# Sigmoid attention with all products in steps of 64 keys of two pairs on four 64x64 parts of TensorE, in native float32, and the mixing on VectorE alone

## The chip, the cores and the metric

The kernel runs on one core of a Trainium2 chip. The metric is the device time of one execution in microseconds (us), the median of three runs. One core has TensorE (PE; its weight loads are shown as PEld), VectorE (DVE), ScalarE (ACT), GpSimd (POOL) and SyncE (SP), whose queue issues every DMA of this kernel.

## The reference

```python
# q, k, v: (8, 12, 448, 64) float32
scores = scale * np.matmul(q, k.transpose(0, 1, 3, 2)) - np.log(S)      # S = 448
attn = 1.0 / (1.0 + np.exp(-scores))
attn_out = np.matmul(attn, v)
x = attn_out.transpose(0, 2, 1, 3).reshape(B, S, H * D)                 # (8, 448, 768)
x_prev = x shifted by one position in the sequence, zeros first
xk = mu_k * x + (1.0 - mu_k) * x_prev
xr = mu_r * x + (1.0 - mu_r) * x_prev
k = np.maximum(xk @ w_k, 0.0)                                           # w_k: float64, 768 x 1024
v = k * k @ w_v                                                         # w_v: float64, 1024 x 768
r = 1.0 / (1.0 + np.exp(-(xr @ w_r)))                                   # w_r: float64, 768 x 768
out = r * v
```

The sigmoid acts on every score alone, so no row of scores has to be complete before its values are used.

## The kernel before

There are 96 heads, taken two at a time: 48 **pairs** `n`, the two heads `h` of a pair on partitions 0-63 and 64-127 of `raw` (q and k, transposed). Two pairs, `n` and `n + 1` with `n` even, are called a **couple** here; there are 24. After the attention comes the channel mix, three matrix products (`xr @ w_r`, `xk @ w_k`, `k*k @ w_v`) written with seven products of half blocks, by line 590. The first two matrices are read as raw float64 bits and made into float32 on VectorE during the attention (`convert`, lines 220 to 224; sums of blocks, line 252; for `w_r` also the split into a high and a low part, lines 297 and 298).

For one pair `n` the attention does this:

- `load`: one DMA brings q and k into `raw[n % 4]`, one brings v into `vn[n % 5]`.
- `prepare` (lines 315 and 316, VectorE): k of the first 384 keys and q are each cast to the fast format fp32r (`hi`), and the remainder `lo` is computed, into a spare part of the weight tiles `slot`.
- `scores` (line 336, TensorE): for each 128 keys and each head three products hi*hi, lo*hi, hi*lo with 64 rows and 128 columns of the array, into `sc`, a ring of three tiles of two PSUM banks.
- `sigmoid` (line 359, ScalarE): one instruction of 128x896 for each 128 keys, `sc` to `pf`, a ring of seven.
- `weigh` (line 366, TensorE): `pf` times v in native float32 with 128 rows and 64 columns, into `av`, two banks.
- The last 64 keys of both pairs of a couple are done together on four 64x64 parts of the array in native float32: `score_tails` (line 347, straight from `raw`), a sigmoid into `pt`, and `weigh_tails` (line 374).
- `gather` (lines 388 to 390): for each of `mu_r`, `mu_k` a memset on GpSimd, a multiplication of the shifted result by 1 - mu on ScalarE (389), then a multiply-add on VectorE (390) and a DMA to DRAM (`xr_d`, `xk_d`); `xo` has four tiles.

The order of all instructions is made by `Plan`: each operation has a cost and a priority, a list scheduler runs them in a model of the engines, and the program is written in the order of the start times. TensorE's operations are also chained by the resource `"order"`, so they stand as written.

Of the kernel before, what the change touches and what calls it, by code (L numbers as in the profile page):

```python
# [8 lines left out]
F32 = mybir.dt.float32  # L9
F32R = mybir.dt.float32r  # L10
AF = mybir.ActivationFunctionType
# [11 lines left out]
class Plan:  # L23
# [7 lines left out]
    def op(self, engine, cost, prio, run, reads, writes, dma=None):  # L31
        i = len(self.ops)
        deps = set()
        for r in reads:
            if r in self.writer:
                deps.add(self.writer[r])
        for w in writes:
            if w in self.writer:
                deps.add(self.writer[w])
            deps.update(self.readers.get(w, ()))  # L40
        for r in reads:
            self.readers.setdefault(r, []).append(i)
        for w in writes:
            self.writer[w] = i
            self.readers[w] = []
        deps.discard(i)
        self.ops.append(Op(engine, cost, prio, run, deps, dma))
# [51 lines left out]
def attention_then_channel_mix(  # L99
# [23 lines left out]
    NT = B * S  # L123
    NJ = DM // P
    NF = DF // P
    NC = S // P
    TAIL = S - NC * P
    KW = NC * P
    QKW = KW + S
    NV = 2 * NC + 1  # L130
    HN = DM // 2
    NJH, NFH = NJ // 2, NF // 2
    WO = NJH * DF // 2
# [21 lines left out]
    wk_o = [dram.tile([P, WO], F32, name=f"wk_o{p}") for p in range(7)]  # L155
    wv_o = [dram.tile([P, WO], F32, name=f"wv_o{p}") for p in range(7)]

    WP, PFB, RAW, WB = 512, 7, 4, 7
    SPARE = 2 * NJH * HN

    def ring(pool, name, bufs, shape, dtype):
        return [pool.tile(shape, dtype, name=f"{name}{i}") for i in range(bufs)]
# [10 lines left out]
    apool = att.enter_context(tc.tile_pool(name="apool", bufs=1, side="right"))  # L173
    ps = ExitStack()
    psum = ps.enter_context(tc.tile_pool(name="psum", bufs=1, space=PSUM))
    av = ring(psum, "av", 2, [P, 512], F32)
    sc = ring(psum, "sc", 3, [P, 2, 512], F32)

    raw = ring(apool, "raw", RAW, [P, 2 * S], F32)
    vn = ring(apool, "vn", 5, [P, NV, D], F32)  # L180
    kk = [slots[g][:, SPARE:SPARE + 2 * KW].rearrange("p (t n) -> p t n", t=2) for g in (0, 3)]
    qh = [slots[g][:, SPARE:SPARE + S] for g in (1, 4)]
    ql = [slots[g][:, SPARE:SPARE + S] for g in (2, 6)]
    pf = ring(apool, "pf", PFB, [P, 2, S], F32)
    pt = ring(apool, "pt", 2, [P, 2, S], F32)
    xo = ring(apool, "xo", 4, [P, S], F32)

    plan = Plan()
    op = plan.op
    SP, PE, ACT, DVE, POOL = "SP", "PE", "ACT", "DVE", "POOL"  # L190
    SWITCH = 200

    def mm(n, cols=S):
        return n * max(cols / 2.4 + 3.5, 205)

    def act(n, sbuf=False, ptr=False):
        return 51 + 0.834 * n + 42 * sbuf + 93 * ptr

    def dve(n, fast=False, ptr=False):
        return 69 + n / (1.92 if fast else 0.96) + 61 * ptr  # L200
# [7 lines left out]
    def dma(dst, src, prio, reads, writes):  # L208
        ns = dst.shape[0] * math.prod(dst.shape[1:]) * 4 / 300
        op(SP, 500, prio, lambda: nc.sync.dma_start(dst, src), reads, writes, dma=ns)  # L210
# [92 lines left out]
        return put  # L303

    def load(n, at):
        dma(raw[n % RAW], qk[n], at, [], [("raw", n % RAW)])
        dma(vn[n % 5], v[n], at, [], [("vn", n % 5)])

    def prepare(n, at):
        i = n % 2  # L310
        src = raw[n % RAW]
        R = ("raw", n % RAW)
        for src_, hi, lo, key in ((src[:, :KW], kk[i][:, 0], kk[i][:, 1], "k"), (src[:, KW:QKW], qh[i], ql[i], "q")):
            w = src_.shape[-1]
            op(DVE, dve(w, True), at, lambda src_=src_, hi=hi: nc.vector.tensor_copy(hi, src_), [R], [(key + "h", i)])  # L315
            op(DVE, dve(w), at, lambda src_=src_, hi=hi, lo=lo: nc.vector.tensor_sub(lo, src_, hi), [R, (key + "h", i)], [(key + "l", i)])  # L316

    half = [slice(h * D, (h + 1) * D) for h in range(2)]

    def pe(cost, go, reads, writes, at):  # L320
        op(PE, cost, at, go, reads, writes + ["order"])

    turns = [0]

    def turn():
        turns[0] += 1
        return (turns[0] - 1) % 3

    def scores(n, c, u, at):
        i = n % 2  # L330
        kc = slice(c * P, (c + 1) * P)

        def go(e):
            qq = (qh, qh, ql)[e]
            for h in range(2):
                nc.tensor.matmul(sc[u][:, h, :S], kk[i][half[h], int(e == 1), kc], qq[i][half[h], :], start=e == 0, stop=e == 2)  # L336

        w = [("sc", u, 0), ("sc", u, 1)]
        pe(mm(1) + SWITCH * (c == 0), lambda: go(0), [("kh", i), ("qh", i)], w, at)
        pe(mm(2), lambda: (go(1), go(2)), [(a, i) for a in ("kh", "kl", "qh", "ql")], w, at)  # L340

    def score_tails(n, u, at):
        def go():
            for m in (n, n + 1):
                t = raw[m % RAW]
                for h in range(2):
                    nc.tensor.matmul(sc[u][half[h ^ (m % 2)], m % 2, :S], t[half[h], QKW:], t[half[h], KW:QKW], start=True, stop=True)  # L347

        pe(752, go, [("raw", m % RAW) for m in (n, n + 1)], [("sc", u, 0), ("sc", u, 1)], at)

    def sigmoid(n, c, u, at):
        if c < NC:
            i = (n * NC + c) % PFB
            f, K = pf[i], ("pf", i)
        else:
            i = n // 2 % 2
            f, K = pt[i], ("pt", i)
        R = [("sc", u, 0), ("sc", u, 1)]
        op(ACT, act(2 * S), at, lambda: nc.scalar.activation(f, sc[u][:, :, :S], AF.Sigmoid, bias=NEG_LOG_S, scale=SCALE), R, [K])  # L359

    def weigh(n, c, at):
        i = (n * NC + c) % PFB

        def go():
            for h in range(2):
                nc.tensor.matmul(av[n % 2][half[h], :S], vn[n % 5][:, h * NC + c, :], pf[i][:, h, :], start=c == 0, stop=False)  # L366

        pe(752 + SWITCH * (c == 0), go, [("pf", i), ("vn", n % 5)], [("av", n % 2)], at)

    def weigh_tails(n, at):  # L370
        def go():
            for m in (n, n + 1):
                for r in range(2):
                    nc.tensor.matmul(av[m % 2][half[r ^ (m % 2)], :S], vn[m % 5][half[r], 2 * NC, :], pt[n // 2 % 2][half[r], m % 2, :], start=False, stop=True)  # L374

        reads = [("pt", n // 2 % 2)] + [("vn", m % 5) for m in (n, n + 1)]
        pe(752 + SWITCH, go, reads, [("av", 0), ("av", 1), ("pair", n)], at)

    nxo = [0]

    def gather(n, at):
        b, j = divmod(n, NP)
        x = av[n % 2]
        for mu, om, dst, key in ((mur, omr, xr_d, "xr_d"), (muk, omk, xk_d, "xk_d")):
            u = nxo[0] % len(xo)
            nxo[0] += 1
            y, Y = xo[u], ("xo", u)
            op(POOL, 200, at - 5, lambda y=y: nc.gpsimd.memset(y[:, 0:1], 0.0), [], [Y])
            op(ACT, act(S, False, True), at, lambda y=y, om=om: nc.scalar.mul(y[:, 1:], x[:, :S - 1], om[:, j:j + 1]), [("av", n % 2), ("om", key)], [Y])  # L389
            op(DVE, dve(S, ptr=True), at - 5, lambda y=y, mu=mu: nc.vector.scalar_tensor_tensor(y, x[:, :S], mu[:, j:j + 1], y, ALU.mult, ALU.add), [("av", n % 2), Y], [Y])  # L390
            dma(dst[b][:, j], y, at - 5, [Y], [(key, n)])


    rr_n = [0]
    used = {}
# [89 lines left out]
        else:  # L485
            operand(stage, 1, key, at)

    load(0, -9)
    prepare(0, -9)
    load(1, -8)  # L490
    load(2, -7)
    for t, src, om, key in ((mur, mu_r, omr, "xr_d"), (muk, mu_k, omk, "xk_d")):
        dma(t, src, -2, [], [("mu", key)])
        op(DVE, 75, 0, lambda t=t, om=om: nc.vector.tensor_scalar(om, t, -1.0, 1.0, ALU.mult, ALU.add), [("mu", key)], [("om", key)])
# [3 lines left out]
    def convert_next(at, after):  # L498
        try:
            work.send((at, after))  # L500
        except StopIteration:
            pass

    def key_chunks(n, at):
        if n + 1 < N:
            prepare(n + 1, at + 0.6 - 5)
        us = [turn() for _ in range(NC)]
        for c in range(NC):
            scores(n, c, us[c], at)
            sigmoid(n, c, us[c], at + 0.1 * c)  # L510

    def last_keys(n, at):
        u = turn()
        score_tails(n, u, at)
        sigmoid(n, NC, u, at + 0.02)

    key_chunks(0, 0)
    last_keys(0, 0)
    for n in range(0, N, 2):
        at = n + 1  # L520
        convert_next(at + 8, n - 2 if n else None)
        key_chunks(n + 1, at)
        if n + 3 < N:
            load(n + 3, at + 0.2 - 5)
        for c in range(NC):
            weigh(n, c, at)
        at = n + 2
        if n + 2 < N:
            key_chunks(n + 2, at)
        for c in range(NC):  # L530
            weigh(n + 1, c, at)
        weigh_tails(n, at)
        if n + 2 < N:
            last_keys(n + 2, at)
        if n + 4 < N:
            load(n + 4, at + 0.2 - 5)
        gather(n, at)
        gather(n + 1, at + 0.05)
    right(0, -1, 0, N - 6)
    right(0, -1, 1, N - 5)  # L540
    with tc.manual_schedule():
# [165 lines left out]
```

## Time and profile before

| | |
|---|---|
| median of three runs | 837.45 us (836.97 to 838.12) |
| the profiled execution | 839.72 us, its span (first to last instruction) 837.8 us |
| attention: first product of line 336 to first product of line 590 | 4.79 to 272.01 us |
| channel mix on TensorE | 272.01 to about 833 us |
| PE busy | 822.5 us, 98% of the span |
| DVE busy | 634.8 us, 76% |
| ACT busy | 468.0 us, 56% |
| mean DMA rate | 214 GB/s |
| granted TensorE clock | 0.997 of full speed |

A matmul's busy time includes its way through the array, and the next one starts before it ends: a busy PE is not a PE at its peak. What a group of matmuls costs is read from the distance between starts, or from the pieces of the chain of work that ended last, which do not overlap.

### The profile page before, as it was taken

Reading aid. Unit: us, or ns where it says so; the run is one execution under the profiler, and the core shown is the slowest. Engines: PE = TensorE matmul, PEld = TensorE weight load, DVE = VectorE, ACT = ScalarE, POOL = GpSimd, SP = SyncE. Lnnn points to the kernel's source line nnn. Section 1 sums busy time; section 2 is a strip of 40 time slices with the busy share of each in tenths; the row PEclk is TensorE's granted clock in tenths of the full one; section 3 lists DMA queues with packets and bytes.
Section 4 is the critical chain, followed back from the end, with each engine's and each line's share of the span. In section 5 each row is a group of like instructions: output and inputs, shape, how many; then the busy total and the mean of one; then the engine's idle time right before and its main releaser. Section 6 shows DMA issues by size and latency. Waiting matters only on the chain.

```text
span 837.8 us, 12701 instructions
## 1 busy us (share of the span) xinstructions
PE 822.5 (98%) x4299; PEld 591.6 (71%) x4299; DVE 634.8 (76%) x1156; ACT 468.0 (56%) x753; POOL 11.0 (1%) x100
## 2 busy tenths in 40 slices
PE   7999999999999999999999999999999999999997
PEld 4444444444444888888888888888888888888886
DVE  5798998787887888889997276386576848949854
ACT  5788978777775444446446646467575233332320
POOL 0000000000000000000000000000000000000000
PEclk9999999999999999999999999999999999999999
DMA  5788867898987965657984527523845465467404
GB/s 206 257 257 292 286 214 229 270 319 295 316 295 234 321 232 199 198 203 239 321 277 159 190 76 247 164 89 127 289 161 204 150 207 175 138 209 219 133 23 155
DMA packets 97489, 179.64 MB, mean 214 GB/s; under 512 B 12560, under 2 KB 53008, under 8 KB 95632
## 3 DMA queue, kind: packets, MB, share of 16 engines
q1 hardware_dynamic: 97424, 178.83, 64.1%
q8 instruction: 34, 0.56, 0.3%
q14 instruction: 31, 0.25, 0.1%
HBM read 109.06 MB, written 69.73 MB: 213 GB/s over the span
## 4 chain that ended last, share of the span: by engine, by line
PE 90%; DMA 5%; ACT 2%; issue 1%; DVE 1%; DVEq 0%; SPq 0%; ACTq 0%; POOL 0%; POOLq 0%
PE xb L590 38%; PE yb L590 29%; PE av L366 11%; PE sc L336 9%; DMA xk_d<-xo 4%; PE av L374 2%; PE sc L347 1%; ACT xo L389 1%; ACT pt L359 1%; ACT pf L359 1%; DVE xo L390 1%; DMA raw<-in_qk 0%; DVE slot L315 0%; ACT rra L451 0%; DVE cc L645 0%
## 5 line engine op out<-in xcount | busy, mean ns | idle before, releaser
L590 PE MATMUL xb<-rra,slot 128*128 128x512 f32 x717 | 173.9, 389 | 0.0
L590 PE MATMUL xb<-rrb,slot 128*128 128x512 f32 x669 | 162.2, 389 | 0.0
L590 PEld LDWEIGHTS xb<-rra,slot 128*128 128x128 f32 x717 | 134.5, 188 | 28.6 <-issue 0.7
L590 PE MATMUL yb<-rra,slot 128*128 128x512 f32 x618 | 150.8, 389 | 0.0
L590 PEld LDWEIGHTS xb<-rrb,slot 128*128 128x128 f32 x669 | 125.6, 188 | 26.0
L359 ACT ACTIVATE pf<-sc 128x896 f32<-128x896 f32 x144 | 123.1, 935 | 25.4 <-PE sc L336 25.4
L590 PEld LDWEIGHTS yb<-rra,slot 128*128 128x128 f32 x618 | 116.0, 188 | 24.1
L366 PE MATMUL av<-pf,vn 128*64 128x448 f32 x576 | 119.6, 551 | 6.0 <-DVE xo L390 6.0
L590 PE MATMUL yb<-rrb,slot 128*128 128x512 f32 x471 | 116.3, 389 | 0.0
L336 PEld LDWEIGHTS sc<-slot,slot 64*128 64x128 f32 x864 | 77.4, 188 | 50.5 <-issue 18.3
L336 PE MATMUL sc<-slot,slot 64*128 64x448 f32 x864 | 107.2, 386 | 4.8 <-DVE slot L315 4.8
L590 PEld LDWEIGHTS yb<-rrb,slot 128*128 128x128 f32 x471 | 88.4, 188 | 18.3
L366 PEld LDWEIGHTS av<-pf,vn 128*64 128x64 f32 x576 | 37.3, 136 | 66.1 <-issue 48.4
L451 ACT CAST rra<-ysa 128x512 fp32r<-128x512 f32 x88 | 52.5, 623 | 48.5 <-PE yb L590 25.9
L452 DVE TENSOR_TENSOR rra<-ysa,rra 128x512 fp32r<-128x512 f32 x76 | 49.4, 685 | 11.0 <-ACT rra L451 10.9
L451 ACT CAST rrb<-ysa 128x512 fp32r<-128x512 f32 x60 | 35.4, 617 | 33.7 <-PE yb L590 11.9
L389 ACT ACTIVATE xo<-av,omr 128x447 f32<-128x447 f32 x48 | 30.7, 639 | 41.5 <-PE av L374 23.4
L316 DVE TENSOR_TENSOR slot<-raw,slot 128x384 fp32r<-128x384 f32 x96 | 52.5, 584 | 0.0
L390 DVE SCALAR_TENSOR_TENSOR xo<-av,mur,xo 128x448 f32<-128x448 f32 x48 | 32.7, 681 | 23.3 <-ACT xo L389 17.5
L452 DVE TENSOR_TENSOR rrb<-ysa,rrb 128x512 fp32r<-128x512 f32 x60 | 39.0, 683 | 9.4 <-ACT rrb L451 9.4
L631 DVE TENSOR_TENSOR u<-yb,p1s 128x512 f32<-128x512 f32 x30 | 20.7, 691 | 32.5 <-PE yb L590 32.2
L576 DVE TENSOR_TENSOR slot<-cc,slot 128x512 fp32r<-128x512 f32 x42 | 28.0, 685 | 19.3 <-ACT slot L575 19.2
(68 smaller groups left out, 790.5 us busy)
## 6 DMA issues: line engine op xcount, KB each, us to landing
raw<-in_qk SPq DMA_DIRECT2D x48, 448.0 KB, 6.2
k_d<-cc SPq DMA_DIRECT2D x56, 256.0 KB, 2.2
vn<-in_v SPq DMA_DIRECT2D x48, 224.0 KB, 2.8
xr_d<-xo SPq DMA_DIRECT2D x48, 224.0 KB, 6.6
xk_d<-xo SPq DMA_DIRECT2D x48, 224.0 KB, 6.3
r_d<-cc SPq DMA_DIRECT2D x42, 256.0 KB, 2.2
out<-cc SPq DMA_DIRECT2D x42, 256.0 KB, 3.1
wraw<-in_moe_w_k SPq DMA_DIRECT2D x12, 512.0 KB, 6.6
```

The costliest lines, as they stand in the source:

```text
L316: op(DVE, dve(w), at, lambda src_=src_, hi=hi, lo=lo: nc.vector.tensor_sub(lo, src_, hi), [R, (key + "h", i)], [(key + "l", i)])
L336: nc.tensor.matmul(sc[u][:, h, :S], kk[i][half[h], int(e == 1), kc], qq[i][half[h], :], start=e == 0, stop=e == 2)
L359: op(ACT, act(2 * S), at, lambda: nc.scalar.activation(f, sc[u][:, :, :S], AF.Sigmoid, bias=NEG_LOG_S, scale=SCALE), R, [K])
L366: nc.tensor.matmul(av[n % 2][half[h], :S], vn[n % 5][:, h * NC + c, :], pf[i][:, h, :], start=c == 0, stop=False)
L374: nc.tensor.matmul(av[m % 2][half[r ^ (m % 2)], :S], vn[m % 5][half[r], 2 * NC, :], pt[n // 2 % 2][half[r], m % 2, :], start=False, stop=True)
L389: op(ACT, act(S, False, True), at, lambda y=y, om=om: nc.scalar.mul(y[:, 1:], x[:, :S - 1], om[:, j:j + 1]), [("av", n % 2), ("om", key)], ...
L390: op(DVE, dve(S, ptr=True), at - 5, lambda y=y, mu=mu: nc.vector.scalar_tensor_tensor(y, x[:, :S], mu[:, j:j + 1], y, ALU.mult, ALU.add), ...
L451: op(ACT, act(TB, True), at, lambda t=t: nc.scalar.copy(hi[:, t], y[:, t]), [Y[t]], [H[t]])
L452: op(DVE, dve(TB), at, lambda t=t: nc.vector.tensor_sub(lo[:, t], y[:, t], hi[:, t]), [Y[t], H[t]], [L[t]])
L576: op(DVE, dve(TB), at, lambda h_=h_, l_=l_, w=w: nc.vector.tensor_sub(l_, w, h_), [W, K + (h, "hi")], [K + (h, "lo")])
L590: nc.tensor.matmul(bank, a, b, start=first and t == 0 and e == 0, stop=t == n - 1 and e == 2, skip_group_check=True)
L631: op(DVE, dve(TB), at, lambda: add(u2[i], y, p1s[i]), [Y, P1], [U2])
```

## The change

`prepare`, `scores` and the separate handling of the last 64 keys go. Each couple now has seven steps of 64 keys. A step is one group of four score products (two pairs, two heads; each of 64 rows, 64 columns and 448 positions, in native float32 from `raw`), one sigmoid of 128x896, and two steps later one group of four products with v. `sc` has two tiles in place of three, `av` four banks in place of two, `pf` four tiles in place of seven, `raw` and `vn` six, `xo` eight. q and k of a pair come in two DMAs, first the first 64 keys with q, then the other keys. The multiplication by 1 - mu moves from ScalarE to VectorE. The host lays q, k and v out accordingly. The channel mix is the same.

```diff
-    WP, PFB, RAW, WB = 512, 7, 4, 7
+    WP, PFB, RAW, WB = 512, 4, 6, 7
-    av = ring(psum, "av", 2, [P, 512], F32)
-    sc = ring(psum, "sc", 3, [P, 2, 512], F32)
+    av = ring(psum, "av", 4, [P, 512], F32)
+    sc = ring(psum, "sc", 2, [P, 2, 512], F32)
...
-    xo = ring(apool, "xo", 4, [P, S], F32)
+    xo = ring(apool, "xo", 8, [P, S], F32)
...
     def load(n, at):
-        dma(raw[n % RAW], qk[n], at, [], [("raw", n % RAW)])
-        dma(vn[n % 5], v[n], at, [], [("vn", n % 5)])
+        i = n % RAW
+        late = 0.5 * (n < 2)
+        for a, c in enumerate((slice(0, D + S), slice(D + S, 2 * S))):
+            dma(raw[i][:, c], qk[n][:, c], at + late * a, [], [("raw", i, a)])
+        dma(vn[i], v[n], at + 2 * late, [], [("vn", i)])
...
+    def score(n, j, t, at):
+        u, f = sc[t % 2], pf[t % PFB]
+        c = slice(0, D) if j == 0 else slice(S + j * D, S + (j + 1) * D)
+        def go():
+            for m in (n, n + 1):
+                x = raw[m % RAW]
+                for h in range(2):
+                    nc.tensor.matmul(u[half[h ^ (m % 2)], m % 2, :S], x[half[h], c], x[half[h], D:D + S], start=True, stop=True)
...
+    def weigh(n, j, t, at):
+        def go():
+            for m in (n, n + 1):
+                for r in range(2):
+                    nc.tensor.matmul(av[bank(m)][half[r ^ (m % 2)], :S], vn[m % RAW][half[r], j, :], pf[t % PFB][half[r], m % 2, :], start=j == 0, stop=j == NV - 1)
...
-            op(ACT, act(S, False, True), at, lambda y=y, om=om: nc.scalar.mul(y[:, 1:], x[:, :S - 1], om[:, j:j + 1]), [("av", n % 2), ("om", key)], [Y])
+            op(DVE, dve(S, ptr=True), at, lambda y=y, om=om: nc.vector.tensor_scalar_mul(y[:, 1:], x[:, :S - 1], om[:, j:j + 1]), [X, ("om", key)], [Y])
...
+    LAG = 2
+    T = N // 2 * NV
+    for t in range(T + LAG):
+        n, j = t // NV * 2, t % NV
+        if t < T:
+            if j == 0:
+                convert_next(n + 8, n - 2 if n else None)
+            score(n, j, t, n + j / NV)
+        if t < LAG:
+            continue
+        n, j = (t - LAG) // NV * 2, (t - LAG) % NV
+        weigh(n, j, t - LAG, n + j / NV)
+        if j == NV - 1:
+            for m in (n, n + 1):
+                gather(m, m)
+                if m + 4 < N:
+                    load(m + 4, n + 0.5)
```

On TensorE, in the middle of the attention, a couple before ends with products of v over 128 rows (`av` from `pf`), the products for the last 64 keys on 64x64 parts (`pt`, `raw`), and then the fp32r scores of the next pair (`slot`); each row stands for two matmuls or, with x4, four:

```order
L366 MATMUL av1_133<-pf4_150,vn2_143 64x448 x2
L366 MATMUL av1_133<-pf5_151,vn2_143 64x448 x2
L366 MATMUL av1_133<-pf6_152,vn2_143 64x448 x2
L374 MATMUL av0_132<-pt1_154,vn1_142 64x448 x2
L374 MATMUL av1_133<-pt1_154,vn2_143 64x448 x2
L347 MATMUL sc2_136<-raw0_137 64x448 x2
L347 MATMUL sc2_136<-raw1_138 64x448 x2
L336 MATMUL sc0_134<-slot4_118,slot3_117 128x448 x4
L336 MATMUL sc0_134<-slot6_120,slot3_117 128x448 x2
L336 MATMUL sc1_135<-slot4_118,slot3_117 128x448 x4
L336 MATMUL sc1_135<-slot6_120,slot3_117 128x448 x2
```

The changed program at the border of two couples (line 315 is the score group, 327 the group with v):

```order
L315 MATMUL sc1_137<-raw0_138 64x448 x2
L315 MATMUL sc1_137<-raw1_139 64x448 x2
L327 MATMUL av2_134<-pf3_153,vn4_148 64x448 x2
L327 MATMUL av3_135<-pf3_153,vn5_149 64x448 x2
L315 MATMUL sc0_136<-raw0_138 64x448 x2
L315 MATMUL sc0_136<-raw1_139 64x448 x2
L327 MATMUL av0_132<-pf0_150,vn0_144 64x448 x2
L327 MATMUL av1_133<-pf0_150,vn1_145 64x448 x2
```

Only groups of one shape are left, a group of scores in turn with a group of v, and a new couple starts in the two banks of `av` that the couple before it does not use.

On ScalarE, where a couple ends, the order before has the four multiplications of `gather` (line 389) around the sigmoid of the last keys (`pt`) and ahead of the next pair's sigmoids:

```order
L389 ACTIVATE xo0_155<-av0_132,omr_65 128x447
L389 ACTIVATE xo1_156<-av0_132,omk_66 128x447
L359 ACTIVATE pt0_153<-sc0_134 128x896
L389 ACTIVATE xo2_157<-av1_133,omr_65 128x447
L389 ACTIVATE xo3_158<-av1_133,omk_66 128x447
L359 ACTIVATE pf5_151<-sc1_135 128x896
```

The changed program in its third couple (line 318 is the sigmoid, 287 the cast of a block of `w_r`, line 297 before):

```order
L318 ACTIVATE pf2_152<-sc0_136 128x896
L287 CAST slot6_120<-wbit_124 128x384
L287 CAST slot2_116<-wbit_124 128x384
L318 ACTIVATE pf3_153<-sc1_137 128x896
L318 ACTIVATE pf0_150<-sc0_136 128x896
```

The multiplications are gone from ScalarE; the casts of the weights stay, in some places two in a row between sigmoids.

More of the change, by code (lines that the diff above doesn't have):

```diff
@@ L125, in attention_then_channel_mix @@
     NF = DF // P
[L126 to L130, printed above, removed]
+    NV = S // D
     HN = DM // 2
@@ L156, in attention_then_channel_mix @@
     wv_o = [dram.tile([P, WO], F32, name=f"wv_o{p}") for p in range(7)]
-    WP, PFB, RAW, WB = 512, 7, 4, 7
-    SPARE = 2 * NJH * HN
+    WP, PFB, RAW, WB = 512, 4, 6, 7
     def ring(pool, name, bufs, shape, dtype):
@@ L175, in attention_then_channel_mix @@
     psum = ps.enter_context(tc.tile_pool(name="psum", bufs=1, space=PSUM))
-    av = ring(psum, "av", 2, [P, 512], F32)
-    sc = ring(psum, "sc", 3, [P, 2, 512], F32)
+    av = ring(psum, "av", 4, [P, 512], F32)
+    sc = ring(psum, "sc", 2, [P, 2, 512], F32)
     raw = ring(apool, "raw", RAW, [P, 2 * S], F32)
[L180 to L183, printed above, removed]
+    vn = ring(apool, "vn", RAW, [P, NV, D], F32)
     pf = ring(apool, "pf", PFB, [P, 2, S], F32)
-    pt = ring(apool, "pt", 2, [P, 2, S], F32)
-    xo = ring(apool, "xo", 4, [P, S], F32)
+    xo = ring(apool, "xo", 8, [P, S], F32)
     plan = Plan()
@@ L190, in attention_then_channel_mix @@
     SP, PE, ACT, DVE, POOL = "SP", "PE", "ACT", "DVE", "POOL"
-    SWITCH = 200
     def mm(n, cols=S):
@@ L305, in load @@
     def load(n, at):
-        dma(raw[n % RAW], qk[n], at, [], [("raw", n % RAW)])
-        dma(vn[n % 5], v[n], at, [], [("vn", n % 5)])
[L309 to L316, printed above, removed]
@@ L318, in attention_then_channel_mix @@
-    half = [slice(h * D, (h + 1) * D) for h in range(2)]
[L320 to L340, printed above, removed]
@@ L342, in score_tails, with pe @@
-    def score_tails(n, u, at):
+        i = n % RAW
[3 more added lines that the diff above has]
+        dma(vn[i], v[n], at + 2 * late, [], [("vn", i)])
+    half = [slice(h * D, (h + 1) * D) for h in range(2)]
+    def pe(go, reads, writes, at):
+        op(PE, 752, at, go, reads, writes + ["order"])
+    def score(n, j, t, at):
+        u, f = sc[t % 2], pf[t % PFB]
+        c = slice(0, D) if j == 0 else slice(S + j * D, S + (j + 1) * D)
@@ L343, in go @@
         def go():
             for m in (n, n + 1):
-                t = raw[m % RAW]
+                x = raw[m % RAW]
                 for h in range(2):
[L347 to L370, printed above, removed]
+                    nc.tensor.matmul(u[half[h ^ (m % 2)], m % 2, :S], x[half[h], c], x[half[h], D:D + S], start=True, stop=True)
+        pe(go, [("raw", m % RAW, a) for m in (n, n + 1) for a in ((0, 1) if j else (0,))], [("sc", t % 2)] + [("pair", n)] * (j == NV - 1), at)
@@ L371, in go, with bank @@
+        op(ACT, act(2 * S), at, lambda: nc.scalar.activation(f, u[:, :, :S], AF.Sigmoid, bias=NEG_LOG_S, scale=SCALE), [("sc", t % 2)], [("pf", t % PFB)])
+    def bank(m):
+        return m % 4
+    def weigh(n, j, t, at):
         def go():
@@ L373, in go @@
                 for r in range(2):
-                    nc.tensor.matmul(av[m % 2][half[r ^ (m % 2)], :S], vn[m % 5][half[r], 2 * NC, :], pt[n // 2 % 2][half[r], m % 2, :], start=False, stop=True)
-        reads = [("pt", n // 2 % 2)] + [("vn", m % 5) for m in (n, n + 1)]
-        pe(752 + SWITCH, go, reads, [("av", 0), ("av", 1), ("pair", n)], at)
+                    nc.tensor.matmul(av[bank(m)][half[r ^ (m % 2)], :S], vn[m % RAW][half[r], j, :], pf[t % PFB][half[r], m % 2, :], start=j == 0, stop=j == NV - 1)
+        reads = [("pf", t % PFB)] + [("vn", m % RAW) for m in (n, n + 1)]
+        pe(go, reads, [("av", bank(m)) for m in (n, n + 1)], at)
     nxo = [0]
@@ L382, in gather @@
         b, j = divmod(n, NP)
-        x = av[n % 2]
+        x, X = av[bank(n)], ("av", bank(n))
         for mu, om, dst, key in ((mur, omr, xr_d, "xr_d"), (muk, omk, xk_d, "xk_d")):
@@ L387, in gather @@
             y, Y = xo[u], ("xo", u)
[L388 to L391, printed above, removed]
+            op(POOL, 200, at, lambda y=y: nc.gpsimd.memset(y[:, 0:1], 0.0), [], [Y])
+            op(DVE, dve(S, ptr=True), at, lambda y=y, om=om: nc.vector.tensor_scalar_mul(y[:, 1:], x[:, :S - 1], om[:, j:j + 1]), [X, ("om", key)], [Y])
+            op(DVE, dve(S, ptr=True), at, lambda y=y, mu=mu: nc.vector.scalar_tensor_tensor(y, x[:, :S], mu[:, j:j + 1], y, ALU.mult, ALU.add), [X, Y], [Y])
+            dma(dst[b][:, j], y, at, [Y], [(key, n)])
     rr_n = [0]
@@ L486, in right @@
             operand(stage, 1, key, at)
[L488 to L491, printed above, removed]
+    for n in range(4):
+        load(n, -9 + n // 2 * 2)
     for t, src, om, key in ((mur, mu_r, omr, "xr_d"), (muk, mu_k, omk, "xk_d")):
@@ L502, in convert_next @@
             pass
[L504 to L538, printed above, removed]
+    LAG = 2
[15 more added lines that the diff above has]
+                    load(m + 4, n + 0.5)
     right(0, -1, 0, N - 6)
@@ L678 @@
     b, h, s, d = inputs["q"].shape
-    full = s // 128
-    main = full * 128
-    pairs = {a: np.asarray(inputs[a]).reshape(b * h // 2, 2, s, d) for a in "qkv"}
-    tail = s - main
     n = b * h // 2
-    vv = np.zeros((n, 128, 2 * full + 1, d), np.float32)
-    vv[:, :, :2 * full] = pairs["v"][:, :, :main].reshape(n, 2, full, 128, d).transpose(0, 3, 1, 2, 4).reshape(n, 128, 2 * full, d)
-    for i in range(n):
-        vv[i, :, 2 * full] = pairs["v"][i, [i % 2, 1 - i % 2], main:].reshape(2 * tail, d)
+    pairs = {a: np.asarray(inputs[a]).reshape(n, 2, s, d) for a in "qkv"}
+    vv = np.stack([pairs["v"][i, [i % 2, 1 - i % 2]].reshape(2, s // d, d, d).transpose(0, 2, 1, 3).reshape(2 * d, s // d, d) for i in range(n)])
     qt, kt = (pairs[a].transpose(0, 1, 3, 2).reshape(n, 2 * d, s) for a in "qk")
     laid = {
-        "qk": np.concatenate([kt[:, :, :main], qt, kt[:, :, main:]], axis=2),
+        "qk": np.concatenate([kt[:, :, :d], qt, kt[:, :, d:]], axis=2),
         "v": vv,
```

## The prediction

> **What bounds the kernel now.** I read the busy times by stretch first, then the chain of work that ended last in order of time, then single groups. Busy us with (count) of PE, PEld, DVE, ACT, POOL, then granted clock, DMA share and GB/s, for the attention, its second part, and the channel mix:
>
> ```profile
> 4.79:272.01 267.22, 261.18 (x1824) 127.04 (x1824) 219.06 (x458) 201.28 (x287) 10.64 (x92) 0.99 0.81 268
> 145.00:272.01 127.01, 123.81 (x864) 59.46 (x860) 101.56 (x204) 90.43 (x125) 5.53 (x48) 0.99 0.85 287
> 272.01:833.40 561.39, 561.34 (x2479) 464.60 (x2475) 413.56 (x694) 265.23 (x464) 0.00 (x0) 1.00 0.57 190
> ```
>
> The channel mix is 561 us in which PE has no gap; it is the same in both kernels. The change can only move the moment at which it starts, 272.01 us. In the attention PE is nearly always busy too, with VectorE at 82% and ScalarE at 75%. The chain in order of time (start us, us, what) shows what a couple consists of:
>
> ```profile
> 117.71 0.91 PE av L374 x8
> 118.62 0.75 PE sc L347 x8
> 119.37 2.23 PE sc L336 x18
> 121.60 2.41 PE av L366 x12
> 124.00 2.02 PE sc L336 x14
> 126.02 2.41 PE av L366 x12
> 128.43 0.91 PE av L374 x8
> ...
> 131.57 0.21 issue
> 131.78 0.66 ACT xo L389
> 133.08 0.04 issue
> 133.13 2.48 PE av L366 x12
> ...
> 140.03 0.91 PE av L374 x8
> ```
>
> From 117.71 to 128.43 the couple is all TensorE: 10.72 us. The next, to 140.03, takes 11.60: the mixing (ScalarE, then VectorE) holds `av`, and line 366 waits for the bank. Over all couples (minimum/median/maximum ns; first and last start us):
>
> ```profile
> L374 PE MATMUL av<-pt,vn x192: 536/562/587, 18.9 to 271.5; 64*64 64x448 f32 x192
> L347 PE MATMUL sc<-raw x192: 536/536/1002, 8.7 to 263.7; 64*64 64x448 f32 x192
> ```
>
> The last start at 271.5 is a second pass, 0.4 after its group's first, so 23 couples lie between 18.9 and 271.1: 10.97 us each. So 0.25 us a couple, 6 us in all, are waits; the rest is TensorE's own work. The waits have a name (us in total, times, longest):
>
> ```profile
> PEld av L366 <- DVE xo L390: 13.5, 23, 2.3
> ...
> DVE wbit L220 <- DMA wraw<-in_moe_w_r: 7.6, 7, 2.4
> ```
>
> **The price of a group on four parts.** The kernel already has both kinds of the new groups once a couple, one behind the other: lines 374 and 347, 8 instructions (four matmuls of two passes). The chain gives 0.75 us for the second of them, which has no change of shape ahead of it. A longer train of passes gives the digits (timeline: start us, us):
>
> ```profile
> 151.49 0.93 PE L347 MATMUL sc<-raw 64*64 64x448 f32 x8
> ...
> 266.44 4.73 PE L366 MATMUL av<-pf,vn 128*64 128x448 f32 x24
> ```
>
> Twelve passes of two matmuls each: 4.73 less the last one's own 0.54 and the first exposed weight load of 0.05 (562 against 536 or 587 in the rows above) is 4.14 for 11 distances, 0.376 a pass, 0.752 a group. The bounds are 0.745 (0.75 rounded) and 0.80 (2.41 / 3, with a change of shape in it); I take 0.752, since the new order never changes shape. Four concurrent parts have the same distance as two: 0.75 in the chain. A couple after is 14 groups: 10.53 us. Before it is 2.23 + 2.02 for fp32r scores, 2 x 2.41 for v, 0.91 + 0.75 for the tails: 10.73. The products themselves gain only 0.2 us a couple, 4.6 in all; what the three fp32r products save over native float32 was paid back in changes of shape and exposed loads, which now go.
>
> **The start.** The chain begins with
>
> ```profile
> 0.73 3.32 DMA raw<-in_qk
> ```
>
> and the timeline goes on
>
> ```profile
> 4.79 3.98 PE L336 MATMUL sc<-slot,slot 64*128 64x448 f32 x18 [4.79 <-DVE slot L315]
> ...
> 6.74 0.67 DVE L315 CAST slot<-raw 128x384 fp32r<-128x384 f32 x2 [0.99 <-DMA raw<-in_qk]
> ...
> 8.71 1.46 PE L347 MATMUL sc<-raw 64*64 64x448 f32 x8
> 10.09 2.09 PE L336 MATMUL sc<-slot,slot 64*128 64x448 f32 x18
> ```
>
> The first 448 KB are there at 4.05, 1,120 KB (two of q and k, one of v, by queue order) at 6.7: 250 KB a us. The first score group after needs the first 256 KB parts of two pairs, 512 KB: 4.3, and no cast, so I start at 4.4 (bounds 4.0 and 5.0). The second parts (896 KB) come at 5.85, when the first group, still slow, ends (5.9); both v (1,344 KB) at 7.6, needed behind three slow groups at 8.9. So no wait for data here. The slow beginning: 3.98 against 2.09 for one pair's scores and 1.46 against 0.93 for line 347 is 2.4 us lost until about 9.5, which I take again as 2.3. *By the Trainium skill ("TensorE: Matmul & The Clock Gate", Part 1) TensorE runs at half rate until about one window of 3.4 us of sustained work is over; the loss would be half of it, 1.7, and the sum 0.6 us less. The row speaks for more, with pauses in the first work that the changed kernel hasn't; I keep the row.*
>
> **What leaves and enters the other engines.** Groups (count | busy us, mean ns | idle before):
>
> ```profile
> L359 ACT ACTIVATE pf<-sc 128x896 f32<-128x896 f32 x144 | 123.1, 935 | 25.4 <-PE sc L336 25.4
> L316 DVE TENSOR_TENSOR slot<-raw,slot 128x384 fp32r<-128x384 f32 x96 | 52.5, 584 | 0.0
> L390 DVE SCALAR_TENSOR_TENSOR xo<-av,mur,xo 128x448 f32<-128x448 f32 x48 | 32.7, 681 | 23.3 <-ACT xo L389 17.5
> L315 DVE CAST slot<-raw 128x384 fp32r<-128x384 f32 x96 | 31.6, 370 | 13.6 <-PE sc L336 8.4 <-DMA raw<-in_qk 5.0
> L389 ACT ACTIVATE xo<-av,omr 128x447 f32<-128x447 f32 x48 | 30.7, 639 | 41.5 <-PE av L374 23.4
> L297 ACT CAST slot<-wbit 128x384 fp32r<-128x384 f32 x21 | 10.8, 547 | 0.0
> ```
>
> VectorE loses the 192 casts and remainders, 84.1 us, and gains 96 multiplications of 447 elements out of PSUM. The trace has none on VectorE; the nearest rows bound one between 0.37 (a cast) and 0.68 (line 390, the same read with a second operand), and I take 0.6, near the latter: 58 us. 219 - 84 + 58 = 193 us of 256: 75%, and no longer ahead of the scores. The mixing of a couple is 8 instructions, at most 8 x 0.68 = 5.4 us; its banks are wanted 10.5 us later, since `av` has four. That removes the wait of line 366; its cover is 5 us. ScalarE loses twice 30.7 us and stays at about 140 of 256. GpSimd's 96 memsets stay. SP issues 48 loads more, and line 388's memset no longer holds an early write, as `xo` has two couples' tiles.
>
> The new tight ring is `sc`: a score group may start when the sigmoid two steps before is done. Its path: 0.93 for the group, 0.94 for the sigmoid, two hand-overs of at most 0.21 (the chain's "issue" above): 2.3 of the two steps' 3.01. Slack 0.7 us. Two casts of line 297 in a row ahead of a sigmoid are 1.1 us and would cost up to 0.4; 21 casts make at most 9 such places, 3.6 us. I take 1.0 for this and all else (0 to 3.6).
>
> **The sum.** 4.4 + 2.3 + 336 x 0.752 = 252.7 + 1.0 + 0.1 (last change of shape) = 260.5 in place of 272.0: 11.5 us earlier, against the profiled execution's own 839.72. That one lies 2.3 above the median of the runs, which I take the difference from: 837.45 - 11.5 = 826.0. That the mix starts as smoothly is covered by VectorE's lighter load; the last couple's mixing (5.4 us) is wanted only by the last blocks.
>
> **The rivals.** (a) *DMA sets the pace in the second part.* DMA issues, KB each, us to landing:
>
> ```profile
> raw<-in_qk SPq DMA_DIRECT2D x48, 448.0 KB, 6.2
> vn<-in_v SPq DMA_DIRECT2D x48, 224.0 KB, 2.8
> xr_d<-xo SPq DMA_DIRECT2D x48, 224.0 KB, 6.6
> wraw<-in_moe_w_k SPq DMA_DIRECT2D x12, 512.0 KB, 6.6
> wk_o<-wbit SPq DMA_DIRECT2D x21, 256.0 KB, 4.4
> ```
>
> A couple there moves 2 x 448 + 2 x 224 + 4 x 224 + 512 + 1.75 x 256 = 3,200 KB, 3.28 MB. At 10.53 us that is 311 GB/s. The row of the second part has 287 at a share of 0.85, so 338 at full share: 92%, and loads are issued two couples ahead. Should it yield 300, a couple takes 10.9 and 12 couples 5 us more: 831. (b) *The gain is all eaten*, if it yields only the 287: 11.4 a couple, 10.7 more, about 837, no change. (c) *Slower, through ScalarE's queue.* A cast of line 297 stands ahead of sigmoids, waits for VectorE, which waits for `wraw`, whose DMA is queued behind four loads at each couple's start. Beyond the slack of 0.7 all of it stops PE. The wait row for `wraw` has up to 2.4 us at a time. At 2 us lost in each of 9 places: 825 + 18 = 843; it decides from 1.4 us a place. Against it: line 297 has no idle time before it now, and `wraw` is asked for a couple ahead. (d) *Parts that share a bank take turns.* Two row parts write one bank of `sc` (and of `av`) at different partitions. If they took turns a group would take 1.5 us and the attention 253 more: about 1079. Line 347 does just this, at 0.75. *The Trainium skill ("TensorEngine Tiling (Array Packing)", Gotcha 1) says that different row tiles cannot access the same PSUM bank at once; the trace disagrees in this form.*
>
> **Chances.** Forecast (822.5 to 829) 0.70; (a) 0.17; (b) 0.05; (c) 0.07; (d) 0.01. The forecast's own lower end: start 4.0, no stalls, 1.7 for the slow beginning gives 824, and the median's own spread 1 more; with (a) the range is 822.5 to 833. A change under 0.2%, 1.7 us, cannot be told from none: faster 0.87, same 0.05, slower 0.08.
>
> **What would show it.** Right: distances of 0.376 us between passes throughout, 10.5 us from couple to couple, the first product of the mix at about 260 us, no wait of TensorE for `xo`, VectorE near 193 us in the attention. Wrong: couples of 10.9 in the second part alone with waits for `raw` or `vn` (a); TensorE waiting for the sigmoid behind casts in the first part (c); passes of 0.75 (d); or a granted clock below 1.00 under nothing but four-part work.

## The result, and the profile after

The changed kernel takes 826.64 us in the median of four runs (826.25 to 827.13), the kernel before 837.46 (836.97 to 838.12): a ratio of 0.9871, interval 0.9854 to 0.9888, 10.8 us less. The forecast was 826.0.

The attention, the channel mix and their engines after, in stretches (busy us and count of PE, PEld, DVE, ACT, POOL; granted clock, DMA share, GB/s):

```profile
3.56:258.37 254.81, 254.81 (x2689) 184.96 (x2689) 198.83 (x361) 165.49 (x198) 8.85 (x88) 1.00 0.85 284
258.37:819.80 561.43, 561.31 (x2477) 464.60 (x2475) 416.21 (x698) 261.79 (x458) 0.00 (x0) 1.00 0.57 190
```

The mix has its 561 us unchanged and begins at 258.4. In the attention PE is busy from the first instruction to the last. The chain of work that ended last, its start and a piece of its middle:

```profile
0.73 2.78 DMA raw<-in_qk
3.56 4.58 PE sc L315 x24
...
103.59 0.75 PE sc L315 x8
105.10 0.75 PE sc L315 x8
105.85 0.75 PE av L327 x8
107.35 0.75 PE av L327 x8
```

There is nothing in it but the first load and groups of 0.75 us; where the kernel before had ScalarE, VectorE and DMA between couples, no piece of another engine is left. (Not every group is listed; the distance from 103.59 to 107.35 is five groups.) The groups over the whole run (minimum/median/maximum ns, first and last start us):

```profile
L327 PE MATMUL av<-pf,vn x1344: 536/536/536, 7.8 to 257.9; 64*64 64x448 f32 x192
L315 PE MATMUL sc<-raw x1344: 536/536/1005, 3.6 to 255.6; 64*64 64x448 f32 x192
```

All 1,344 instructions of line 327 took 536 ns, where 562 was the median of line 374: no weight load is exposed any more. Only scores at the very start are slow (1005).

### The profile page after: what moved, and what is told of

Its sections match the earlier page's. It is cut to its first block, busy times and chain, and to the rows that moved or that the text cites. A ratio compares the mean times of both kernels' runs of the same rounds, so it can differ in the third digit from the quotient of the medians.

```text
span 824.5 us, 14185 instructions
## 1 busy us (share of the span) xinstructions
PE 816.1 (99%) x5163; PEld 649.6 (79%) x5163; DVE 616.4 (75%) x1060; ACT 428.8 (52%) x657; POOL 9.4 (1%) x100
## 4 chain that ended last, share of the span: by engine, by line
PE 99%; DMA 0%; DVE 0%; issue 0%
PE xb L522 38%; PE yb L522 30%; PE sc L315 16%; PE av L327 15%; DMA raw<-in_qk 0%; DVE cc L577 0%; DVE cc L547 0%
## 5 line engine op out<-in xcount | busy, mean ns | idle before, releaser
L318 ACT ACTIVATE pf<-sc 128x896 f32<-128x896 f32 x168 | 154.0, 917 | 90.7 <-PE sc L315 90.3
L315 PE MATMUL sc<-raw 64*64 64x448 f32 x1344 | 187.9, 541 | 3.6 <-DMA raw<-in_qk 3.6
L327 PE MATMUL av<-pf,vn 64*64 64x448 f32 x1344 | 185.9, 536 | 0.0
L315 PEld LDWEIGHTS sc<-raw 64*64 64x64 f32 x1344 | 92.4, 134 | 39.0 <-DMA raw<-in_qk 5.0
L327 PEld LDWEIGHTS av<-pf,vn 64*64 64x64 f32 x1344 | 92.5, 133 | 33.7 <-ACT pf L318 0.4
L404 DVE TENSOR_TENSOR rra<-ysa,rra 128x512 fp32r<-128x512 f32 x76 | 49.9, 686 | 11.1 <-ACT rra L403 10.9
L342 DVE TENSOR_SCALAR xo<-av,omr 128x447 f32<-128x447 f32 x48 | 32.5, 678 | 31.8 <-PE av L327 31.7
L508 DVE TENSOR_TENSOR slot<-cc,slot 128x512 fp32r<-128x512 f32 x42 | 28.0, 686 | 18.7 <-ACT slot L507 18.6
L561 ACT COPY p1s<-xb 128x512 f32<-128x512 f32 x30 | 17.6, 588 | 37.9 <-PE xb L522 37.9
L541 ACT ACTIVATE cc<-cc 128x512 f32<-128x512 f32 x56 | 35.3, 631 | 1.0
```

The lines of the kernel that those rows point to most:

```text
L315: nc.tensor.matmul(u[half[h ^ (m % 2)], m % 2, :S], x[half[h], c], x[half[h], D:D + S], start=True, stop=True)
L318: op(ACT, act(2 * S), at, lambda: nc.scalar.activation(f, u[:, :, :S], AF.Sigmoid, bias=NEG_LOG_S, scale=SCALE), [("sc", t % 2)], [("pf", ...
L327: nc.tensor.matmul(av[bank(m)][half[r ^ (m % 2)], :S], vn[m % RAW][half[r], j, :], pf[t % PFB][half[r], m % 2, :], start=j == 0, stop=j == ...
L342: op(DVE, dve(S, ptr=True), at, lambda y=y, om=om: nc.vector.tensor_scalar_mul(y[:, 1:], x[:, :S - 1], om[:, j:j + 1]), [X, ("om", key)], [Y])
L404: op(DVE, dve(TB), at, lambda t=t: nc.vector.tensor_sub(lo[:, t], y[:, t], hi[:, t]), [Y[t], H[t]], [L[t]])
L508: op(DVE, dve(TB), at, lambda h_=h_, l_=l_, w=w: nc.vector.tensor_sub(l_, w, h_), [W, K + (h, "hi")], [K + (h, "lo")])
```

## The experiments

Each kernel is compared with the one that it was made from; later differences in us are against the changed kernel's 826.64. The kernel before varies more than the changed one: 835 to 843 us over the runs beside the experiments, the changed kernel's near variants (four tiles of `xo`, products ahead of the start) stay within 1.1 us.

**The kernel before, once more.**

> The kernel before, unchanged, profiled once more. Its first profiled execution (839.72 us, mix from 272.0) was 2.3 us over the median of its unprofiled runs. If the pause of TensorE around 252 to 260 us in that trace was of that execution alone, the mix begins near 270 us here and the span is about 835.5; if it belongs to the order of the program, the mix begins at 272 again and the span is 837.8.

837.2 us, span 835.3. Its tails start and end at

```profile
L374 PE MATMUL av<-pt,vn x192: 536/562/587, 18.6 to 269.1; 64*64 64x448 f32 x192
```

and the mix at 269.5, 2.5 us earlier than in the first trace. The pause around 252 us is in both: line 366 waits 1.93 us there and 1.91 here, so it belongs to the order of the program. What differs most is the granted clock (third number from the right in the rows by stretch) just behind it. First the first trace, then this one:

```profile
254.10 3.43 PE L366 MATMUL av<-pf,vn 128*64 128x448 f32 x12 [1.93 <-DVE xo L390]
255.00:260.00 5.00, 5.00 (x28) 2.60 (x24) 4.93 (x10) 1.31 (x3) 0.34 (x3) 0.66 0.63 236
```

```profile
253.21 2.48 PE L366 MATMUL av<-pf,vn 128*64 128x448 f32 x12 [1.91 <-DVE xo L390]
255.00:260.00 5.00, 5.00 (x34) 2.38 (x30) 4.90 (x9) 2.54 (x3) 0.30 (x3) 1.00 0.54 178
```

At a granted clock of 0.66 this group and the next took 6.0 us (254.10 to 260.14) in place of 4.5 (253.21 to 257.67): 1.6 of the 2.5 us. The other 0.9 had come in smaller waits before 254 us. So the change moved the mix by 11.1 us in an ordinary run, not by 13.6. A couple before is (269.1 - 0.4 - 18.6) / 23 = 10.87 us on average.

**Seven tiles of `xo` in the kernel before.**

```diff
-    xo = ring(apool, "xo", 4, [P, S], F32)
+    xo = ring(apool, "xo", 7, [P, S], F32)
```

> The kernel before with seven tiles of xo in place of four (and one pt in place of two, which its order allows for nothing). Theory: the 6 us of waits in the attention before are for xo, whose four tiles are held until the writes to DRAM have landed; then 832 to 834.5 us. Rival: the two banks of av hold the next pair until both engines of the mixing are through, whatever xo does; then 837.5 within 1.7.

(`pt` goes from two tiles to one with it.) 834.35 us, 0.9963 (0.9943 to 0.9983) of before: about 3 us less, mix from 266.9. Waits of line 366 for the mixing stay. Those of the products (PE) and of their weight loads (PEld), first in the kernel before (the second trace), then here:

```profile
PEld av L366 <- DVE xo L390: 12.8, 23, 2.3
PE av L366 <- DVE xo L390: 5.0, 7, 1.9
```

```profile
PEld av L366 <- DVE xo L390: 10.7, 23, 1.7
PE av L366 <- DVE xo L390: 3.2, 3, 1.3
```

So `xo` was a part of the waits, some 2.6 us against the 269.5 of an ordinary run. What is left waits for the same mixing with `xo` to spare; that the two banks of `av` are the whole of it is likely, but not shown by itself. **Four tiles of `xo` in the changed kernel** is the same question from the other side:

> The changed kernel with four tiles of xo in place of eight. Theory: with four banks of av the mixing of a couple may wait for the landing of the writes of the couple before, 4 us and ended by then, without holding TensorE: 826 to 828. Rival: four tiles hold the mixing as they did before: 829 to 833.

826.74 us, mix from 258.6: the eight tiles bring nothing once `av` has four banks.

**Two banks of `av` in the changed kernel** (and three tiles of `sc`):

```diff
-    av = ring(psum, "av", 4, [P, 512], F32)
-    sc = ring(psum, "sc", 2, [P, 2, 512], F32)
+    av = ring(psum, "av", 2, [P, 512], F32)
+    sc = ring(psum, "sc", 3, [P, 2, 512], F32)
```

> The changed kernel with two banks of av in place of four, and three tiles of sc in place of two in the banks set free. Theory: four banks are what takes the mixing off TensorE's path: with two, each couple's first group of v waits for the eight instructions of the mixing before, some 5 us less one group of scores, 4 to 4.5 us x 23 couples: 918 to 930. Rival: the order finds other work meanwhile, and the loss is under 15 us: 827 to 842.

929.68 us in one run, mix from 361.8, 103 us later; the waits (us in total, times, longest):

```profile
PEld av L327 <- DVE xo L343: 48.9, 23, 2.2
PEld av L327 <- ACT pf L318: 43.3, 23, 2.8
PE av L327 <- DVE xo L343: 31.0, 23, 1.4
```

Four banks are indispensable to this form. The loss is 4.5 us a couple on average, but not all of it is waiting: in most couples TensorE loses 1.7 us to a wait for a sigmoid (`pf`, the loop runs empty) and 2.0 to the wait for the bank, 3.7 together, 85 us over 23 couples. Up to 15 us more go by an estimate to the clock: granted were 0.97, 0.95 and 0.96 in the stretches from 0 to 100, 100 to 200 and 200 to 362 us, where the changed kernel has 1.00.

**VectorE's multiplication in the kernel before.**

> The kernel before with the multiplication by 1 - mu on VectorE, and nothing else of the change. Theory: the move gains nothing by itself and only becomes possible when the casts go: VectorE has 219 us of work in 267 and gets 96 x 0.6 = 58 more, so the attention grows by at least 10 us: 848 to 870. Rival: ScalarE's multiplications ahead of the sigmoids are what held TensorE, and the move alone gives a gain: 831 to 836.

846.0 us in one run. Its attention:

```profile
4.67:270.67 266.00, 257.28 (x1825) 128.50 (x1825) 257.93 (x534) 153.87 (x195) 12.42 (x92) 1.00 0.80 259
```

VectorE is busy for 258 of 266 us. The attention loses only 1.1 us; the rest comes out in the mix, which takes 7.7 us longer since work for it is late:

```profile
ACT rrb L451 <- DMA ysa<-xr_d: 22.7, 1, 22.7
PEld xb L590 <- ACT cc L603: 4.1, 2, 2.5
PEld xb L590 <- ACT p1s L629: 3.6, 1, 3.6
```

The theory had the sign and the cause, but its 848 to 870 us was too high, and it put the loss into the wrong stage. In this one run the move alone is a loss.

**ScalarE's multiplication in the changed kernel.**

```diff
-            op(DVE, dve(S, ptr=True), at, lambda ...: nc.vector.tensor_scalar_mul(...
+            op(ACT, act(S, False, True), at, lambda ...: nc.scalar.mul(...
```

> The changed kernel with the multiplication by 1 - mu back on ScalarE. Theory: ScalarE has 0.5 to 0.6 us free in each step of 1.5, and a multiplication of 0.64 delays a sigmoid by less than the slack of two sc tiles; where the multiplications run is of no weight: 826 to 829. Rival: four of them per couple hold up the sigmoids as before, 0.25 us a couple: about 832.6.

838.50 us, 1.0007 (0.9995 to 1.0019) of before. Both expectations fell: the whole gain is gone. The timeline of ScalarE at the border of two couples, and TensorE's next score group:

```profile
151.57 0.63 ACT L342 ACTIVATE xo<-av,omr 128x447 f32<-128x447 f32 x1
152.09 0.64 ACT L342 ACTIVATE xo<-av,omk 128x447 f32<-128x447 f32 x1
152.60 0.64 ACT L342 ACTIVATE xo<-av,omr 128x447 f32<-128x447 f32 x1
153.12 0.65 ACT L342 ACTIVATE xo<-av,omk 128x447 f32<-128x447 f32 x1
153.63 1.75 ACT L318 ACTIVATE pf<-sc 128x896 f32<-128x896 f32 x2
...
154.63 0.98 PE L315 MATMUL sc<-raw 64*64 64x448 f32 x8 [0.24 <-ACT pf L318]
```

Four multiplications stand in a row ahead of a sigmoid, 2.1 us against a slack of under 1 us; the group that `sc` holds back starts at 154.63 in place of 154.21 (the group before it began at 153.46). From couple to couple it is 11.0 us in place of 10.53: over 23 couples 11 of the 12 us. Whether the engine or the row of four is to blame, the next one tells.

**The same, spread** (priority `at + 6` in place of `at`, so that one or two stand between sigmoids):

> The changed kernel with the multiplication by 1 - mu on ScalarE as in a_actmul (838.5 us), but with a later priority, so that the four of a couple stand between sigmoids (two, one, one) and not four in a row ahead of one. Theory: a_actmul lost 0.5 us a couple since four multiplications, 2.1 us, stand ahead of a sigmoid with 0.8 us of slack; ScalarE has room for them one or two at a time, and the loss goes: 826 to 829. Rival: any multiplication on ScalarE costs, since it takes 4 x 0.53 us a couple from an engine whose sigmoids are the other half of TensorE's loop: 833 to 838.5.

827.30 us, 0.9864 (0.9844 to 0.9884) of before, mix from 259.3. It is the order, not the engine: ScalarE has room for the multiplications, one or two at a time.

**One step of lag in place of two** (`LAG = 1`):

> The changed kernel with the group of v one step behind the scores in place of two (LAG = 1). The way from the start of a score group to its finished sigmoid now has 2.26 us (three groups) in place of 3.76. Theory (the trace after: score at 10.03, its sigmoid ends at 12.18, so 2.2 with the hand-over): it just fits, 826 to 831. Rival (the bounds of the prediction, 2.3 and casts in between): 0.05 to 0.1 us lost in each of 168 steps, 835 to 843.

831.23 us, 4.6 more. In the steady part it just fits: the group with v waits for its weights until 0.2 us before its turn (weight load and group in the timeline):

```profile
150.43 0.38 PEld L327 LDWEIGHTS av<-pf,vn 64*64 64x64 f32 x8 [0.37 <-ACT pf L318]
150.66 0.93 PE L327 MATMUL av<-pf,vn 64*64 64x448 f32 x8
```

Of the 4.2 us by which the mix starts later, 0.9 lie in the slow start and 0.5 at the end, where the last group waits for the last sigmoid. The others lie in single places (0.05 to 0.9 us), the larger of them where casts of the weights or of the mix's first operands stand ahead of a sigmoid.

**Work on TensorE ahead of the first scores** (24 instructions on zeros, from 1.18 to 3.64 us):

> The changed kernel with three groups of products of zeros in the scores' shape (256, 256 and 192 columns, 2.1 to 2.6 us) on TensorE while the first loads are under way. Theory: the attention takes 254.9 us for 252.7 us of groups, and the 2.1 between are a slow TensorE at its start; work ahead of the first scores moves the end of the slow time forward by some 2 us, and 1 to 2 us are gained: 824.6 to 825.7. Rival: the first groups are slow since their data come late: no change, 826.6 within 0.7.

826.45 us, mix from 258.0, 0.35 earlier: no difference that can be told. But the trace shows that the slow passes did go. In the changed kernel a pass takes 0.92 to 1.0 us up to the one that starts at 6.2, and 0.54 from 7.2 on; with work ahead it takes 0.54 to 0.59 from 4.8 on. What holds TensorE then is the loads of `raw`:

```profile
5.34 0.20 PEld L323 LDWEIGHTS sc<-raw 64*64 64x64 f32 x4 [0.78 <-DMA raw<-in_qk]
6.06 0.57 PEld L323 LDWEIGHTS sc<-raw 64*64 64x64 f32 x10 [0.53 <-DMA raw<-in_qk]
```

So theory and rival are both right: slow passes and late loads lie over each other in the 2.1 us that the attention takes beyond its groups, and taking away the first leaves the second.

**A change of shape, priced by itself.** After each score group one product of 16 columns, once over 128 rows, once on a 64x64 part:

```diff
+            nc.tensor.matmul(u[:D, 0, S:S + 16], wz, wz[:, :16], start=True, stop=True)          # a_shape
+            nc.tensor.matmul(u[:D, 0, S:S + 16], wz[:D], wz[:D, :16], start=True, stop=True)     # a_small
```

> The changed kernel with one more small product per step (16 columns, zeros, written beside the scores and not read) that uses 128 rows of the array, so that the array changes shape twice in each of 168 steps. Theory: a change of shape costs 0.1 to 0.2 us with the weight load that it exposes; 168 x (2 x 0.1 to 0.2 + 0.05) = 42 to 75 us more: 868 to 902. Rival: changes of shape cost nothing, the pauses in the kernel before were waits: as a_small, within 3 us.

> The control to a_shape: the same small product per step on a 64x64 part, so without a change of shape. Theory and rival: 168 x 0.03 to 0.1 us more, 832 to 843.

890.13 and 847.12 us, one run each. The step, from score group to score group, first with the change of shape, then without:

```profile
151.21 0.93 PE L317 MATMUL sc<-raw 64*64 64x448 f32 x8
152.07 0.29 PE L318 MATMUL sc<-wz 128*64 128x16 f32 x2
152.29 0.98 PE L330 MATMUL av<-pf,vn 64*64 64x448 f32 x8
153.09 0.93 PE L317 MATMUL sc<-raw 64*64 64x448 f32 x8
```

```profile
151.21 0.97 PE L317 MATMUL sc<-raw 64*64 64x448 f32 x8
152.83 0.97 PE L317 MATMUL sc<-raw 64*64 64x448 f32 x8
```

1.88 against 1.62, and 1.50 without either. Two changes cost 0.26 us a step: 43.0 us over 336 changes, 0.128 us each, the mean of the two directions. This takes the small product itself to cost the same on 128 rows as on 64.

**More DMA in the changed kernel** (v loaded a second time into tiles that nothing reads):

> The changed kernel with v loaded a second time into tiles that nothing reads, 448 KB more per couple. In the second part of the attention a couple then moves 3.74 MB, 355 GB/s at 10.53 us. Theory: DMA has room up to about 338 GB/s (287 at a share of 0.85 in the trace before), so a couple takes 11.1 there and 12 of them 5 to 8 us more, with waits of TensorE for raw or vn: 831 to 835. Rival: DMA has more room or the loads two couples ahead carry it through: 826 to 828.

839.87 us, 13 more, which is over both expectations. But the attention ends 0.9 us later only (mix from 259.3), at 321 GB/s and a share of 0.95 in its first half; the loss is in the mix:

```profile
286.65 1.66 ACT L405 CAST rrb<-ysa 128x512 fp32r<-128x512 f32 x3 [26.95 <-DMA ysa<-xr_d]
...
288.85 1.65 PE L524 MATMUL xb<-rrb,slot 128*128 128x512 f32 x3 [4.72 <-ACT cc L537]
```

The DMAs fall behind during the attention without holding it, and what is read for the mix's first steps stands at the end of the queue: these reads are issued at 279.6 to 283.3 us, in the changed kernel at 263.6 to 267.7. TensorE waits 4.7 us ahead of 288.85 and 3.2 ahead of 299.95. The other 4.7 us of the mix's loss are not waiting: around the end of each of these waits the granted clock falls (third number from the right), and products that take 6.28 us in the changed kernel take 7.89 from 288.85 on.

```profile
275.00:300.00 25.00, 17.07 (x69) 13.24 (x67) 17.08 (x33) 10.22 (x20) 0.00 (x0) 0.91 0.84 289
300.00:350.00 50.00, 50.00 (x209) 41.14 (x210) 46.64 (x86) 23.73 (x43) 0.00 (x0) 0.94 0.62 214
```

The changed kernel itself is near this edge:

```profile
272.51 1.66 ACT L403 CAST rrb<-ysa 128x512 fp32r<-128x512 f32 x3 [13.76 <-DMA ysa<-xr_d]
273.16 1.90 DVE L404 TENSOR_TENSOR rrb<-ysa,rrb 128x512 fp32r<-128x512 f32 x3 [3.51 <-ACT rrb L403]
276.88 1.30 PE L522 MATMUL yb<-rrb,slot 128*128 128x512 f32 x5
```

The operand is ready at 275.1 and used at 276.9: 1.8 us of room.

## Why the prediction came out

- **The group of 0.752 us** held: five groups from 103.59 to 107.35 are 3.76. 336 of them, 252.7 us, are the attention's 254.8 but for 2.1 at the start. Rival (d), parts that share a bank, is out with 2,688 instructions at this distance.
- **The waits that go** held: between couples none is left, and with two banks of `av` waits of 3.7 us a couple appear. Which ring held TensorE before is now known in part: `xo` for about 2.6 us. The size, 0.25 us a couple or 6 us, was read with two errors. The last of the 23 couples has no scores of a next pair and takes only 8.6 us, and 1.6 us were the clock; without both, the trace has 6.2 us of waits, an ordinary run 5.6. That 6 came out is luck.
- **What the fp32r products save is paid back in changes of shape** was argued; a price is now measured, for one kind of change and in the changed kernel. A couple before has five changes (scores, v, scores, v, tails, scores), if all cost alike 0.64 us of its 10.72. Without them its products would be 10.1, less than the 10.53 of the new form. By this estimate the products' own gain comes of being of one shape, not of doing less.
- **The account of the gain** in an ordinary run: the first product 1.15 us earlier (3.56 against 4.71); 24 couples at 10.53 in place of 10.72, 4.6 us; the waits, 5.6 us (250.0 between the first and the last tails, less 22 x 10.72 and 8.54 for the last couple). These are 11.3; the 0.2 over the 11.1 is the slow start, 2.1 after against 1.9 that is left for it before. So half of the gain is the waits. No run has the old products with four banks of `av`; how much of the 5.6 us they would give by themselves stays open.
- **Terms mis-sized.** The start was put at 4.4 and came at 3.56: not the rate was wrong (both first parts of 256 KB were there at 4.15, forecast 4.3), but the first group doesn't need both. Its first pair's products start when that pair's part lands, the second pair's at 4.20. The stalls, put at 1.0, were none, which leaves nothing of rivals (b) and (c). ScalarE was put at about 140 us busy in the attention and had 165.5; with the multiplications off it this did no harm. The forecast's attention ended at 260.5, the real one at 258.4, 2.1 us too late; the trace of before ended 2.5 us later than an ordinary run's, most of it the clock of 0.66, which the prediction didn't look for. The two errors hid each other: the difference of the two profiled executions would have been 13.6, not 11.5. That 826.0 is within 0.7 us of the result is luck to this extent: with either error alone it would have been 828.5 or 823.9.
- **The slow start**, 2.3 taken and 2.1 found, is slow passes over late loads. The passes are at full speed 3.7 us after the first one, and work ahead moved this from 7.2 to 4.8 us; the loads then hold the groups, and only 0.35 us is gained. "No wait for data here" was not quite right: the second parts of `raw` landed at 5.35 and 5.87, as forecast (5.85), but the weight loads of the second group had waited up to 0.9 us for them.
- **What the prediction didn't see** is where ScalarE's multiplications stand. It counted 61 us leaving an engine that had room, and put the worth into four banks. With them left where the planner sets them the gain is nil; the slack of 0.7 us that it worked out for two casts would have told that four multiplications (2.1 us) don't fit.
- **The mix's start** was called covered by VectorE's lighter load. VectorE was lighter (198.8 us; 193 forecast), but the cover hangs on DMA, and 1.8 us of it are left. Rival (a) had the resource right and the place wrong: TensorE wouldn't wait for `raw` or `vn` but for the mix's first operands.

## What to carry to other kernels

Count the changes of shape on TensorE before its multiply-adds: here groups of one shape with more passes beat a mixture that needs fewer. A tight ring is fed by what stands in the queue of the engine that frees it, so the worst row of foreign instructions, not that engine's share, has to fit the slack; a planner's priority can be worth as much as the whole change. And a trace of one execution can be 0.3% off: take the profile of the reference twice before a difference of two profiles is trusted, and read the granted clock in stretches of 5 us. The mean of 0.997 hid a stretch at 0.66.

## What the runs showed of the hardware

A change between a 64x64 and a 128x64 shape costs 0.128 us, if the small product costs the same in both, and a product of 16 columns in native float32 on one part 0.12 us a step (20.5 us over 168). Four concurrent 64x64 parts keep 0.376 us a pass with two row parts writing one bank at different partitions. A multiplication of 447 float32 elements from PSUM takes VectorE 0.677 us, as long as the multiply-add with a second operand (0.675), where 0.6 had been assumed; back to back the starts are 0.6 apart. At the start of work TensorE's passes take up to 1.9 times as long (1.0 us against 0.54), until 3.7 us after the first one in the changed kernel and 3.6 with work ahead, while the granted clock reads 1.00. Later the granted clock falls behind some waits of TensorE: to 0.66 over 5 us behind one of 1.9 us in the first trace of the kernel before, and behind those of 4.7 and 3.2 us in the run with more DMA. It didn't fall behind a wait of 1.9 us at the same place in the second trace.
